# A new order of work on all five engines, and new engines for the casts, in a fused attention and gated feed-forward kernel

## The chip, the cores and the metric

The kernel runs on one core of a Trainium2 chip. A core has five engines, each with its own queue of instructions that it works off strictly in the order in which they were written: TensorE (PE in the profile) for matmuls, VectorE (DVE), ScalarE (ACT), GpSimd (POOL), and SyncE (SP), which here only issues DMAs. Sixteen DMA engines move data between the device memory and the on-chip memory SBUF. Matmuls write into PSUM, a second on-chip memory, from where VectorE or ScalarE must take the results away.

The metric is the device time of one execution in microseconds (us). The kernel before was timed in three runs: 247.0, 247.38 and 248.49 us, median 247.38 us.

## The reference

The inputs are q, k and v of shape (8 batches, 8 heads, 576 positions, 64) in float32, a forget factor f of shape (8, 8, 576), and the weights w_in (512 x 1024), conv_w (3 x 1024) and w_out (1024 x 512).

```python
def _attn_ref(q, k, v, f):
    scale = 1.0 / np.sqrt(D)
    scores = scale * np.matmul(q, k.transpose(0, 1, 3, 2))
    log_f = np.log(np.clip(f, 0.0001, 1.0))
    cum = np.cumsum(log_f, axis=-1)
    decay = cum[:, :, :, None] - cum[:, :, None, :]
    causal = np.triu(np.ones((S, S), dtype=bool), k=1)
    scores = np.where(causal, -1000000000.0, scores + decay)
    scores = scores - np.max(scores, axis=-1, keepdims=True)
    attn = np.exp(scores)
    attn = attn / (np.sum(attn, axis=-1, keepdims=True) + 1e-09)
    return np.matmul(attn, v)

def _moe_ref(x, w_in, conv_w, w_out):
    h = np.maximum(x @ w_in, 0.0)
    hp = np.concatenate([zeros, h, zeros], axis=1)      # one position on each side
    conv_out = sum(conv_w[k] * hp[:, k:k + S, :] for k in range(3))
    gate = 1.0 / (1.0 + np.exp(-conv_out))
    return (h * gate) @ w_out
```

The output of the attention, heads side by side, is the input x of the feed-forward part (FFN). Both are computed for each of the 8 batches.

## The kernel before, in words

The attention is cut into 16 half batches, numbered 0 to 15, of four heads each. The FFN runs per batch, over eight blocks of 128 hidden channels (ff 0 to 7). Everything is written as named tasks, about a thousand of them; a table in the source, ORDER, lists them in one long sequence, and `Plan.play` walks through it and writes the instructions of each task to its engine. So ORDER alone sets the order on each engine's queue, SP's included. A name with an @ behind it also chooses the engine where the kernel allows several (casts of v, casts of the weights, copies out of PSUM).

The tasks, with the half batch or batch as the first number in the name:

- Loads by SP: `ld` loads q and k of half batches 0 and 1 in plain form (L159); `q` loads q or k of half batches 2 to 15 with a transposing DMA (L180, 576 KB in float32, 28 of them); `v` loads v (L209, five pieces a batch); `wi` and `wo` load the weights (L510).
- Casts and small work: `tp` transposes the plain q and k on TensorE (L166) and `cl` takes them from PSUM (L172 on ACT, L174 on DVE); for the transposed loads `cl` clears two of each pair of rows in place (L186 on DVE, half batches 2 to 7). `rw` (L202, L203) or, from half batch 8 on, `fi` (L194, L196) then writes the decay rows into the loaded tile by DMA, from an image that `ki` (L279) made. Only after `rw` or `fi` has landed can the scores of that half batch begin. `va` casts v to float16 (L217, and L219 for its last 64 rows), `wic` and `woc` cast the weights (L518).
- Scores on TensorE: per pair of heads `sd` (diagonal blocks, numbered 2 x half batch and 2 x half batch + 1) and two `so` (the blocks below it), per half batch `st` (the last 64 positions), all L312; where the causal mask is added on TensorE (half batches 0 to 7) a mask matmul (L320) comes first; half batch 0 adds the decay by two more matmuls per block (L315, L317). ScalarE takes the exponentials: `ed` (L353), `eo` (L370), `et` (L332). From half batch 8 on GpSimd sets the masked part to zero: `md` (L356), `mt` (L335).
- `pv` (L389, L394) multiplies with v, in two parts; `n` and `m` on DVE (L403, L405) divide by the row sums; `t` (L414) turns the result on TensorE and `tx` (L417) takes it from PSUM, or a transposing DMA `tx` does both (L420, half batches 11 to 15).
- FFN: `f` (L429) is x @ w_in for one ff; `r` (L440, ACT) the relu; `c` and `d` (L446, L448, DVE) the three-point convolution; `a` (L451, ACT) the gate's tanh or sigmoid; `g` (L458 or L456, DVE) the product; `o` (L474) is the product with w_out; `e` (L479, L484) copies it from PSUM and `s` (L490, L495, L497, L499, L500) stores it.

PSUM holds four buffers (`ps`) that all of these share: a TensorE task that takes one must wait until the engine that reads it out has released one. The loaded q and k lie in a ring of four tiles, so the loads of half batch n wait for the last scores of half batch n-4.

## Time and profile before

| what | before |
|---|---|
| median of 3 runs | 247.38 us (247.0 to 248.49) |
| span of the profiled execution | 244.1 us (244.06 to two places), 6385 instructions |
| median of the runs less that span | 3.3 us |
| PE busy | 226.9 us (93%) |
| ACT busy | 206.9 us (85%) |
| DVE busy | 205.1 us (84%) |
| POOL busy | 52.9 us (22%) |
| DMA queue of SP | 119981 packets, 48.97 MB, 92.4% of 16 engines' span |

The page gives no time of the profiled execution other than its span, from the first instruction to the last; the 3.3 us by which the median of the runs is longer lies around the span. Busy times are sums over one execution; an engine can be busy on work on which nothing waits. The share of the DMA queue is the time that its packets took, against 16 engines for the whole span.

### The profile page before, as it was taken

The numbers are of one execution on the slowest core, as the hardware profiler recorded it, in microseconds if no ns is written. First come the engines' busy times: TensorE is split into PE (matmuls) and PEld (weight loads), VectorE is DVE, ScalarE is ACT, GpSimd is POOL, SyncE is SP. The second block draws the span as 40 slices with busy tenths as digits, with TensorE's granted clock in tenths as the row PEclk, the third lists the DMA queues.
The fourth block names the chain that finished last, engine by engine and source line by source line (L and its number), as shares of the span: only waits on it lengthen the run. The fifth ranks groups of instructions, "written<-read, shape, count | busy, mean of one in ns | idle before, by whom it ended". The sixth has DMA issues, their size and how long they took to land.

```text
span 244.1 us, 6385 instructions
## 1 busy us (share of the span) xinstructions
PE 226.9 (93%) x2627; PEld 145.0 (59%) x2627; DVE 205.1 (84%) x323; ACT 206.9 (85%) x278; POOL 52.9 (22%) x77
## 2 busy tenths in 40 slices
...
GB/s 192 328 159 243 304 204 192 202 253 279 204 188 205 228 158 240 229 314 186 198 256 246 187 209 257 273 134 222 194 260 188 236 140 3 168 157 62 142 86 216
DMA packets 120176, 49.68 MB, mean 204 GB/s; under 512 B 109759, under 2 KB 110271, under 8 KB 120147
## 3 DMA queue, kind: packets, MB, share of 16 engines
q1 hardware_dynamic: 119981, 48.97, 92.4%
...
q10 hardware_dynamic: 166, 0.31, 0.4%
...
HBM read 21.11 MB, written 10.17 MB: 128 GB/s over the span
## 4 chain that ended last, share of the span: by engine, by line
PE 78%; DVE 7%; DMA 6%; ACT 4%; issue 1%; ACTq 1%; SPq 1%; DVEq 0%
PE ps L474 24%; PE ps L429 20%; PE ps L312 15%; PE ps L389 7%; DMA qk<-in_q_dram 3%; PE ps L320 3%; PE ps L394 3%; PE ps L166 2%; PE ps L414 2%; DVE u L446 2%; ACT pp L370 2%; DMA pd<-in_moe_conv_w_dram 2%; DVE u L448 2%; DVE qk L186 1%; DMA qk<-image 1%
## 5 line engine op out<-in xcount | busy, mean ns | idle before, releaser
L429 PE MATMUL ps<-xt,w_in_f 128*128 128x512 f16 (+1 forms) x512 | 69.9, 286 | 0.0
L370 ACT ACTIVATE pp<-ps 128x1024 f16<-128x1024 f32 x64 | 64.7, 1032 | 4.2 <-PE ps L312 2.7
L474 PE MATMUL ps<-w_out_f,hg 128*128 128x512 f16 x288 | 66.8, 379 | 0.0
L312 PE MATMUL ps<-qk 128*128 128x128 bf16 (+2 forms) x576 | 63.4, 240 | 1.6 <-ACT pp L353 0.8
L446 DVE SCALAR_TENSOR_TENSOR u<-ht,cwt 128x576 f32<-128x576 f16 x64 | 52.7, 837 | 3.6 <-ACT ht L440 3.4
L451 ACT ACTIVATE hg<-u,cw 128x576 f16<-128x576 f32 x64 | 48.7, 782 | 5.9 <-DVE u L448 5.8
L448 DVE SCALAR_TENSOR_TENSOR u<-ht,cwt,u 128x576 f32<-128x576 f16 x64 | 53.2, 846 | 0.5
L429 PEld LDWEIGHTS <-w_in_f 128*128 128x128 f16 x512 | 34.3, 98 | 28.5
L312 PEld LDWEIGHTS <-qk 128*128 128x128 bf16 x576 | 39.2, 98 | 19.8 <-issue 3.3
L440 ACT ACTIVATE ht<-ps 128x576 f16<-128x576 f32 x64 | 41.0, 663 | 6.0 <-DVE hg L458 2.7
L474 PEld LDWEIGHTS <-hg 128*128 128x128 f16 x288 | 26.9, 98 | 28.8
L458 DVE SCALAR_TENSOR_TENSOR hg<-hg,ht 128x576 f16<-128x576 f16 x51 | 38.7, 771 | 0.6 <-ACT hg L451 0.5
L356 POOL TENSOR_SCALAR_AFFINE_SELECT pp<-pd 128x1024 f16<-128x1024 f32 x16 | 19.7, 1244 | 53.6 <-ACT pd L353 53.6
L389 PE MATMUL ps<-va,pp 128*128 128x65 f16 x640 | 24.8, 193 | 1.1 <-DVE va L217 1.0
L389 PEld LDWEIGHTS <-pp 128*128 128x128 f16 x640 | 22.6, 97 | 3.7 <-DVE va L217 1.3
L405 DVE TENSOR_TENSOR xm<-ps,rc 128x896 f16<-128x896 f32 (+1 forms) x32 | 23.9, 751 | 0.5
L353 ACT ACTIVATE pp<-ps 128x1024 f16<-128x1024 f32 x16 | 16.6, 1039 | 4.7 <-PE ps L312 3.9
L353 ACT ACTIVATE pd<-ps 128x1024 f32<-128x1024 f32 x16 | 16.2, 1023 | 1.2 <-PE ps L312 1.0
L217 POOL CAST va<-vf 128x1024 f16<-128x1024 f32 x8 | 10.0, 1252 | 32.1 <-DMA vf<-in_v_dram 27.8
L320 PE MATMUL ps<-mask,ident 128*128 128x512 bf16 (+1 forms) x40 | 14.3, 359 | 1.5 <-ACT pp L370 0.8
L403 DVE RECIPROCAL rc<-ps 128x14 f32<-128x14 f32 (+1 forms) x32 | 6.7, 208 | 8.6 <-PE ps L394 5.5
L479 ACT COPY ob<-ps 128x1024 f32<-128x1024 f32 (+1 forms) x14 | 12.9, 919 | 0.3 <-issue 0.2
...
## 6 DMA issues: line engine op xcount, KB each, us to landing
...
```

What stands on the lines that cost most here:

```text
L312: nc.tensor.matmul(o, tk[:, h * S + k0:h * S + k0 + 128], tq[:, h * S + q0:h * S + q0 + n], start=first, stop=last and not by_matmul(hb, h))
L353: nc.scalar.activation(o, ps_of(f"sd{i}").rearrange("p (s c) -> p s c", s=2), AF.Exp, scale=SCALE)
L370: nc.scalar.activation(pair(i)[:, s, 512:1536], ps_of(f"so{i}.{s}"), AF.Exp, scale=SCALE)
L389: nc.tensor.matmul(ps[:, c:c + D + 1], block(hb, h, m, n), va[:, h, m, 0:D + 1], start=(m == 0), stop=(m == n))
L405: nc.vector.tensor_tensor(xm[:, CUT * D * u:CUT * D * u + nj * k * D].rearrange("p (j x d) -> p j x d", x=k, d=D), got[:, :, :, 0:D], r.un ...
L429: nc.tensor.matmul(ps[:, t0:t1], w_in_f16[:, cc, 128 * ff:128 * (ff + 1)], xt[:, cc // 2, x:x + t1 - t0], start=(cc == 0), stop=(cc == NCC ...
L440: nc.scalar.activation(ht_of(b, ff)[:, 2:2 + S], ps_of(f"f{b}.{ff}")[:, 0:S], AF.Relu, scale=1.0 if (b, ff) in LATE else 0.5)
L446: nc.vector.scalar_tensor_tensor(u, ht[:, 1:1 + S], cwt[:, ff, 0:1], ht[:, 2:2 + S], op0=ALU.mult, op1=ALU.add)
L448: nc.vector.scalar_tensor_tensor(u, ht[:, 3:3 + S], cwt[:, ff, 1:2], u, op0=ALU.mult, op1=ALU.add)
L451: nc.scalar.activation(hg_of(b, ff), u_t[slot[f"c{b}.{ff}", "u"]], AF.Sigmoid if (b, ff) in LATE else AF.Tanh, scale=cw[:, ff, 1:2])
L458: nc.vector.scalar_tensor_tensor(hv, hv, 1.0, ht_of(b, ff)[:, 2:2 + S], op0=ALU.add, op1=ALU.mult)
L474: nc.tensor.matmul(ps[:, 512 * (c % 2):512 * (c % 2 + 1)], w, w_out_f16[:, ff, :], start=(ff == 0), stop=(ff == NFF - 1))
```

## The change

Only the table ORDER changes. It holds the same 1054 tasks, and each task does what it did. Their sequence is new throughout, and 39 tasks of a free choice run on another engine:

| kind of task | before | after |
|---|---|---|
| `va`, 128 x 1024 | POOL 8, ACT 4, DVE 4 | POOL 13, ACT 1, DVE 2 |
| `va`, 64 x 256 | POOL 6, ACT 6, DVE 4 | POOL 12, ACT 1, DVE 3 |
| `wic`, `woc` | POOL 8 | POOL 6, ACT 1, DVE 1 |
| `cl` of half batches 0 and 1 | ACT 5, DVE 3 | ACT 7, DVE 1 |
| `tx` from PSUM | DVE 9, ACT 2 | DVE 10, ACT 1 |
| `e`, 1024 wide | ACT 11, DVE 3 | ACT 13, DVE 1 |
| `e`, 512 wide | ACT 6, DVE 2 | ACT 6, DVE 2 |

The diff is one line of the table for another; its beginning:

```diff
 ORDER = """
-dca cw ld0 ld1 ld0.0.0 tp0.0.0 dcl ld0.1.0 ld0.0.1 tp0.0.1 tp0.1.0 v0.0 ld0.1.1 ld1.0.1 ld1.0.0 dcs dck v0.1 v0.2 v0.3 v0.4
...
+ld0 ld1 ld0.0.1 ld1.0.0 ld0.0.0 ld1.0.1 tp1.0.0 dca q2.1 tp0.0.0 tp1.0.1 tp0.0.1 dcl cl0.0.1@ACT ld0.1.0 cl1.0.1@ACT cl0.0.0@ACT
...
 """
```

What this does to the queues is shown at three places.

**The start of ScalarE's queue.** The rows follow the logarithm of f and its table load. qk_85 and qk_86 are the tiles of half batches 0 and 1; L172 is `cl`, L353 `ed`, L370 `eo`. Before:

```order
L172 ACTIVATE qk_85<-ps_130,lim 128x1152
L172 ACTIVATE qk_85<-ps_131,lim 128x1152
L172 ACTIVATE qk_85<-ps_132,lim 128x1152
L353 ACTIVATE pp_95<-ps_131 128x2x512
L370 ACTIVATE pp_95<-ps_132 128x1024
L370 ACTIVATE pp_95<-ps_131 128x1024
```

And after the change:

```order
L172 ACTIVATE qk_85<-ps_132,lim 128x1152
L172 ACTIVATE qk_86<-ps_131,lim 128x1152
L172 ACTIVATE qk_85<-ps_130,lim 128x1152
L172 ACTIVATE qk_86<-ps_131,lim 128x1152
L172 ACTIVATE qk_86<-ps_132,lim 128x1152
L172 ACTIVATE qk_86<-ps_129,lim 128x1152
L353 ACTIVATE pp_95<-ps_130 128x2x512
L172 ACTIVATE qk_85<-ps_129,lim 128x1152
L370 ACTIVATE pp_95<-ps_130 128x1024
```

Three casts stood ahead of the first exponential; now six do, four of them for half batch 1, and a seventh follows.

**SP's queue between the decay rows of two half batches.** qk_86, qk_87 and qk_88 are the tiles of half batches 5, 6 and 7 here; L202 and L203 together are one `rw`. Before, from `rw5` to the beginning of `rw6`:

```order
L202 DMA qk_86<-image 1x2304
L203 DMA qk_86<-image 2x2304
L510 DMA ob_128<-in_moe_w_out_dram 128x2x512
L180 DMA_TRANSPOSE qk_87<-in_q_dram 128x2304
L180 DMA_TRANSPOSE qk_87<-in_k_dram 128x2304
L180 DMA_TRANSPOSE qk_88<-in_q_dram 128x2304
L180 DMA_TRANSPOSE qk_88<-in_k_dram 128x2304
L209 DMA vf_90<-in_v_dram 128x8x64 x2
L202 DMA qk_87<-image 1x2304
```

After, the stretch that ends with `rw6`; the rows before the first L202 are a load for half batch 5, a piece of v, and the first load for half batch 6:

```order
L180 DMA_TRANSPOSE qk_86<-in_q_dram 128x2304
L209 DMA vf_89<-in_v_dram 128x8x64
L180 DMA_TRANSPOSE qk_87<-in_q_dram 128x2304
L202 DMA qk_86<-image 1x2304
L203 DMA qk_86<-image 2x2304
L209 DMA vf_89<-in_v_dram 128x8x64 x2
L180 DMA_TRANSPOSE qk_87<-in_k_dram 128x2304
L209 DMA vf_89<-in_v_dram 128x8x64
L180 DMA_TRANSPOSE qk_88<-in_q_dram 128x2304
L202 DMA qk_87<-image 1x2304
L203 DMA qk_87<-image 2x2304
```

The transposing loads stood four in a row; now a plain load stands between two of them nearly everywhere, and all four loads of w_out come behind `rw6`, where three of them stood ahead of `rw5` and one behind it.

**The end of SP's queue.** The stores of the last two batches; L490 and the last L497 (or L499 with L500) belong to batch 7. Before:

```order
L495 DMA out_dram<-ob_126 128x2x512
L495 DMA out_dram<-ob_125 128x2x512
L499 DMA out_dram<-ob_128 64x512
L500 DMA out_dram<-ob_128 64x512
L490 DMA out_dram<-ob_127 128x512 x2
L490 DMA out_dram<-ob_126 128x512 x2
```

After:

```order
L495 DMA out_dram<-ob_128 128x2x512
L495 DMA out_dram<-ob_125 128x2x512
L490 DMA out_dram<-ob_126 128x512
L490 DMA out_dram<-ob_127 128x512 x2
L490 DMA out_dram<-ob_126 128x512
L497 DMA out_dram<-ob_128 128x512
```

The last store was one of 256 KB behind two copies out of PSUM; now it is the last block of the batch, in one DMA, behind one copy.

2 lines of the change are left out of this document (1 added, 1 removed).

## The prediction

> **What bounds the kernel now.** I read the page's busy times first, then the table of stretches, then the chain that ended last, then SP's queue.
>
> ```profile
> PE 226.9 (93%) x2627; PEld 145.0 (59%) x2627; DVE 205.1 (84%) x323; ACT 206.9 (85%) x278; POOL 52.9 (22%) x77
> ...
> 0.00:10.00 10.00, 2.83 (x27) 2.85 (x28) 5.69 (x23) 3.98 (x4) 5.37 (x31) 1.00 0.85 243
> ...
> 20.00:30.00 10.00, 8.82 (x111) 6.29 (x109) 4.25 (x5) 7.30 (x10) 3.06 (x3) 1.00 0.97 275
> ...
> 40.00:60.00 20.00, 16.67 (x247) 11.51 (x246) 19.79 (x30) 19.47 (x28) 4.29 (x4) 1.00 1.11 242
> 60.00:100.00 40.00, 39.99 (x485) 25.72 (x483) 38.17 (x57) 38.20 (x54) 5.52 (x5) 1.00 1.06 204
> ...
> 230.00:244.00 14.00, 8.66 (x41) 3.72 (x38) 4.82 (x9) 4.73 (x7) 0.00 (x0) 0.99 0.39 132
> ```
>
> Columns of a stretch: length, then busy time (and instructions) of PE, weight loads, DVE, ACT, POOL, then TensorE's granted clock, the DMA share and GB/s. PE is busy 226.9 of 244.06 us. Its idle 17.2 us lie in four places: 7.17 us before 10 us, 1.18 in 20 to 30, 3.33 in 40 to 60, and 5.34 at the end. From 60 us until the last matmul PE has no hole worth naming, at a granted clock of 1.00. So a new order of the same matmuls can win or lose in the first 60 us and at the tail, or lose by new holes behind.
>
> A busy PE need not be a fast one, so I price the tasks by the chain, where pieces follow each other without overlap:
>
> ```profile
> 33.81 0.50 PE ps L414 x9
> ...
> 60.32 0.22 PE ps L320
> 60.54 0.22 PE ps L312 x4
> ...
> 62.18 0.44 PE ps L312 x4
> 62.62 0.98 PE ps L429 x8
> ...
> 69.25 1.73 PE ps L474 x8
> ...
> 77.48 0.99 PE ps L389 x32
> ...
> 83.30 0.44 PE ps L394 x20
> 83.74 0.32 PE ps L320
> ```
>
> Prices: `t` and `tp` 0.50, `so` 0.44, a masked `sd` 4 x 0.22 = 0.88, `f` 0.98, `o` 1.73, `pv` 0.99 and 0.69 (eight L389 at a quarter of 0.99, and 0.44). 83.74 is `sd13`, the first score of half batch 6. PE's work ahead of it: 15.0 for what both orders open with (eight `tp` 4.0, the weights of the convolution 0.9, half batch 0 with three matmuls where others have one 10.1), ten masked `sd` 8.8, twenty `so` 8.8, five `st` 1.1, `pv` 0 to 4 and half of 5 9.4, four `t` 2.0, sixteen `f` 15.7, four `o` 6.9: together 67.7. **PE's lag**, the clock less the work done, is 83.7 - 67.7 = 16.0 us there, and hardly grows until the end. The forecast is a forecast of this lag and of the tail.
>
> What made the lag? In 40 to 60 us ACT (19.47 of 20) and DVE (19.79) are full and PE is not. SP's queue is the other suspect:
>
> ```profile
> 54.81 6.16 SPq L209 DMA_DIRECT2D vf<-in_v_dram  x4
> ...
> 62.15 0.38 SPq L202 DMA_DIRECT2D qk<-image  x1
> ...
> 63.77 3.96 SPq L180 DMA_TRANSPOSE qk<-in_q_dram  x1
> ...
> 77.27 1.14 SPq L209 DMA_DIRECT2D vf<-in_v_dram  x2
> ...
> 85.65 6.12 SPq L180 DMA_TRANSPOSE qk<-in_k_dram  x2
> ...
> 96.95 0.95 SPq L194 DMA_DIRECT2D qk<-blank  x1
> ...
> 115.29 4.33 SPq L180 DMA_TRANSPOSE qk<-in_k_dram  x2
> ```
>
> SP issues without a gap. Four transposing loads took 77.27 - 63.77 = 13.5 us, four others 96.95 - 85.65 = 11.3 us: 2.8 to 3.4 us each, and 2.2 us where nothing held them back (4.33 for two). Four pieces of v took 6.16, 1.5 each. So the transfers are a queue nearly as full as PE, and what an order puts ahead of a needed one is paid.
>
> **The change, part by part.** (1) *The start.*
>
> ```profile
> GB/s 0 28 288 311 210 306 262 271 357 394 390 308 228 218 217 165 183 4 198 292 122 286 256 244 250 296 330 301 346 321 138 186 286 162 212 256 110 79 290 228
> ...
> 9.26 3.72 ACT L172 ACTIVATE qk<-ps,lim 128x1152 uint16<-128x1152 uint16 x3
> ...
> 11.83 0.38 PE L320 MATMUL ps<-mask,ident 128*128 128x512 bf16 x1
> ...
> 22.71 3.01 DMA qk<-image
> ```
>
> The first line gives what the DMAs moved in each of the first 40 us; its first nine slices add up to 2.03 MB. Before, `sd0` (11.83) waited for the first plain loads and three casts on ACT, 3.72 us. After, the first cast needs `tp0.0.1`, which stands behind `tp1.0.1` on PE, and so four loads of 1.77 MB beside the 0.29 MB of f: about 9 us, plus two turns, 10.2 us. Six casts at 1.24 end at 17.7, and `sd0` can begin after the third, at about 14. Half batch 1 then needs `rw1`; its image DMA took 3.01 us. Behind the casts that is 17.7 + 3.5, and with one more transposing load ahead of it in SP's queue up to 23, against 25.7 before. But PE has then done only 11.4 us (`tp` 4.0, two `sd` and three `so` of half batch 0 7.4), so the lag is 22.5 - 11.4 = 11 already: the earlier decay rows win nothing, since PE's other work was put behind them. **No lag below 11 us is to be had.**
>
> (2) *The decay rows of half batch 6.* After, PE's work ahead of `sd12` is 15.0 + ten `sd` 8.8 + twenty `so` 8.8 + four `st` 0.9 + `pv` 0 to 3 and half of 4 7.7 + four `t` 2.0 + eleven `f` 10.8 = 54.0: five `f`, four `o` and some `pv` less than before, so q, k and v are needed earlier against the clock. In SP's queue `rw6` has ahead of it what `rw5` had (issued at 62.15), plus three transposing loads and one `rw` (1.0), less one piece of v (1.5) and three loads of w_out; such a load costs between 0.5 (its issue below) and 1.3 us (512 KB at the best slice, 394 GB/s).
>
> ```profile
> 23.45 1.43 SPq L510 DMA_DIRECT2D ob<-in_moe_w_in_dram  x3
> ```
>
> With 2.8 us for a transposing load: 62.15 + 8.4 + 1.0 - 1.5 - (1.5 to 3.9), 66.2 to 68.5, and 3.5 until landed: 69.7 to 72.0, middle 70.8; lag 16.8. With 3.4 us: up to 73.8, lag 19.8. With 2.2 us for all eleven (6.6 for the three, and eight older ones 0.8 cheaper each by the 3.0 that they had): 6 to 8 us earlier, and the start's 11 to 12 us rule. I take 2.8, the price of the less crowded four, since the change puts plain loads between: **+0.8 us** of lag, with ends -4 and +3.8.
>
> The DMA: Bandwidth & Descriptors page of the Trainium skill (section Latency and other measured facts) gives a DMA transpose 261 GB/s, so by an estimate 590 KB would take 2.3 us. By that the lag would be the start's, the faster rival's. The trace's 2.8 to 3.4 us speak against it in runs of four.
>
> (3) *Engines of casts.*
>
> ```profile
> L479 ACT COPY ob<-ps 128x1024 f32<-128x1024 f32 x11 | 11.0, 1003 | 0.3 <-issue 0.2
> ...
> L172 ACT ACTIVATE qk<-ps,lim 128x1152 uint16<-128x1152 uint16 x5 | 6.3, 1308 | 0.1
> ...
> L174 DVE TENSOR_SCALAR qk<-ps,lim 128x1152 uint16<-128x1152 uint16 x3 | 4.4, 1477 | 4.7 <-PE ps L166 4.6
> L217 ACT CAST va<-vf 128x1024 f16<-128x1024 f32 x4 | 4.3, 1074 | 0.0
> ...
> L479 DVE COPY ob<-ps 128x1024 f32<-128x1024 f32 x3 | 3.7, 1218 | 2.0 <-ACT xt L417 1.9
> L217 DVE CAST va<-vf 128x1024 f16<-128x1024 f32 x4 | 3.6, 908 | 0.4 <-DMA out_dram<-ob 0.4
> ...
> L219 ACT CAST va<-vf 64x256 f16<-64x256 f32 x6 | 2.4, 408 | 0.0
> ```
>
> DVE loses two big `va` (1.8), two `cl` (3.0) and two `e` (2.4) and gains a weight cast (0.9) and a `tx` (0.8): -5.5 us of 205. ACT loses three big and five small `va` (3.2 + 2.0) and a `tx` (about 1.1), and gains two `cl` (2.6), a weight cast (1.1) and two `e` (2.0): -0.6. POOL gains five big and six small `va` and loses two weight casts. The price at the end is 0 as long as PE is full behind 60 us; without that cover DVE's 5.5 us would count.
>
> ```profile
> 65.26 1.50 POOL L217 CAST va<-vf 128x1024 f16<-128x1024 f32 x1 [4.25 <-PE ps L429]
> ...
> 65.05 0.81 DVE L446 SCALAR_TENSOR_TENSOR u<-ht,cwt 128x576 f32<-128x576 f16 x1
> 66.37 1.00 DVE L446 SCALAR_TENSOR_TENSOR u<-ht,cwt 128x576 f32<-128x576 f16 x1 [0.51 <-ACT ht L440]
> ...
> 16.53 1.04 POOL L217 CAST va<-vf 128x1024 f16<-128x1024 f32 x1 [10.07 <-DMA vf<-in_v_dram]
> ```
>
> A cast on POOL takes 1.04 alone and 1.50 where DVE's L446 began 0.2 us ahead of it, and the next L446 ran 0.19 longer while the cast ended: each makes the other wait. Eleven casts more, at 1.04 (and some 0.4 for a small one), less two, can hold DVE up by 5.5 us at most: DVE's gain is then gone, no more. The SBUF — State Buffer page of the Trainium skill (section SBUF: two separate sides) calls the port pair that the two share an exclusive lock, the loser fully blocked; the rows agree, and by that rule the sum stays as it is.
>
> (4) *The tail.*
>
> ```profile
> 226.41 12.25 PE L474 MATMUL ps<-w_out_f,hg 128*128 128x512 f16 x56
> ...
> 238.69 1.07 ACT L484 COPY ob<-ps 128x512 f32<-128x512 f32 x2 [0.45 <-PE ps L474]
> ```
>
> Behind the last matmul two copies stand on ACT (1.07), then a store. After, one copy of the last block does: **-0.5 us**. -0.7 if the smaller store lands sooner; 0 if `e7.3` is late and pushes `e7.4`.
>
> **Sum**, against the profiled execution: 244.06 + 0.8 - 0.5 = 244.4 us of span. The median of the runs lies 3.3 us above the span of the profile before, so 247.7 us: no change that can be told.
>
> **Rivals.** *A, the forecast*: the lag is 15 to 18 and the time 245 to 249.8. *B, faster*: a transposing load with plain loads behind it costs near 2.2 us, and the full queues of 40 to 60 us are spread, since the new order brings half batches 3 to 5 ahead of much of the FFN of batch 0. For it: 2.2 us occurs, and the runs of four are what is broken up. Against it: the start's 11. Lag 12.5, 3.5 less than now, and the tail: 247.4 - 4.0 = 243.4 us. *C, slower*: `rw6` (and with the same arithmetic `fi8` and `fi10`) comes late, because a transposing load ahead of it that half batch 6 doesn't need (`q7.0`) delays it in SP's strict order, and PE waits at `sd12`. It decides from 3.2 us a load; at 3.4 the lag is 19.8: 247.4 + 3.8 - 0.5 = 250.7 us. For it: SP has no gap to catch up in, and PE is ahead of the clock by less work. *D, the change doesn't do what it says*: the mutual waits of GpSimd and DVE aren't removed but multiplied by the 25 casts there, and reach PE through a late `m` or `va`. If half of the 5.5 us gets through: 250 us. Against it: DVE is relieved by as much.
>
> **Chances.** A 0.42, B 0.31, C 0.21, D 0.06. Faster by over 1% (below 244.9) is B, 0.31; slower by over 1% (above 249.9) is C and D, 0.27; within 1%, about what a measurement here can tell from no change, 0.42. The range goes from somewhat below B's time to above C's, as the ends of step 2 are far apart: 242.2 to 252.0; A's own is 245 to 249.8.
>
> **What would show it.** The stretch 0 to 10 with PE still near 3 us busy; `sd0` at about 14; the first L312 of half batch 1 at 21.5 to 23; SP without gaps and `rw6` issued at 66 to 69; PE full from about 72 us; no L484 pair behind the last matmul. The prediction is wrong if PE shows holes behind 75 us (a new wait, on ACT's or DVE's order or a late `va`), or if `rw6` is issued before 63.

## The result and the profile after

| | before | after |
|---|---|---|
| median | 247.31 us (247.0 to 248.49, 4 runs) | 265.89 us (264.46 to 267.09, 4 runs) |
| span of the profiled execution | 244.06 us | 262.7 us |
| DVE's busy time until 60 us, and behind it | 41.34 and 163.74 us | 29.08 and 182.82 us |

The ratio is 1.073, 95% interval 1.067 to 1.079: **7% slower**, far outside the range of 242.2 to 252.0. The same quantity as in the prediction, PE's lag (the clock less the work done, by the prediction's prices), shows when it happened: 19.2 us at 60 us (before 15.4), 26.6 at 100 (15.9), 29.5 at 150 (16.1), 35.5 at 220 (16.5). So 3.8 us were lost in the first 60 us and 15.2 more behind them, in the part where the prediction held PE to be full. Medians and ratios here and below leave out runs in a slower state of the chip, one of experiment 10 (255.61 us) and four of before. The kernel before, timed anew beside the experiments, had medians of 247.1 to 248.0 us, so differences below some 1 us tell nothing.

First the busy times of the page, the shares of the chain that ended last by engine, and the table of stretches of after (columns as in the prediction):

```profile
PE 234.4 (89%) x2627; PEld 148.3 (56%) x2627; DVE 211.9 (81%) x318; ACT 208.6 (79%) x274; POOL 63.6 (24%) x86
PE 40%; DVE 26%; ACT 10%; DMA 9%; SPq 8%; issue 4%; POOL 2%; DVEq 0%; ACTq 0%; POOLq 0%
...
0.00:60.00 60.00, 47.84 (x612) 36.46 (x613) 29.08 (x61) 44.10 (x49) 13.61 (x41) 0.97 1.00 210
60.00:262.00 202.00, 186.57 (x2018) 111.80 (x2014) 182.82 (x258) 164.48 (x225) 49.95 (x45) 0.99 0.82 184
...
60.00:80.00 20.00, 18.59 (x224) 12.21 (x221) 19.93 (x30) 18.54 (x25) 3.40 (x3) 1.00 0.80 188
80.00:100.00 20.00, 17.26 (x193) 10.36 (x191) 17.73 (x24) 13.78 (x19) 5.52 (x6) 0.91 0.95 217
100.00:120.00 20.00, 18.05 (x212) 11.04 (x211) 19.67 (x26) 17.06 (x25) 5.58 (x6) 1.00 1.12 200
```

and of before the chain's shares and the stretches, cut in the same way:

```profile
PE 78%; DVE 7%; DMA 6%; ACT 4%; issue 1%; ACTq 1%; SPq 1%; DVEq 0%
...
0.00:60.00 60.00, 48.32 (x671) 36.66 (x672) 41.34 (x79) 45.98 (x55) 16.17 (x42) 1.00 1.07 236
60.00:244.00 184.00, 178.55 (x1959) 108.36 (x1956) 163.74 (x245) 160.94 (x224) 36.76 (x36) 1.00 0.89 193
```

What is to be seen: PE was busy as long until 60 us (47.84 against 48.32, of it 3.41 us at half clock after the change), but **DVE 12.3 us less**. In the three stretches from 60 us on DVE is 89 to 100% busy (19.93, 17.73 and 19.67 of 20) while PE has holes (18.59, 17.26, 18.05), and the chain that ended last runs through DVE for 26% of the span instead of 7%. The last matmul ended at 238.7 before and at 257.7 after. From 60 us to there DVE was busy for 163.74 of 178.7 us before, 92%, and for 182.82 of 197.7 after, 92% again. DVE has 19.1 us more to do behind 60 us, and the span is 18.6 us longer. That suggests DVE, but busy time alone doesn't show what PE waited for; the waits and the experiments below test it.

Why had it 19.1 us more? 12.3 were left over from the first 60 us. The other 6.8 are a longer sum, 211.9 against 205.1, although casts and copies worth 5.5 us were taken from it. The groups of DVE's three long element operations (count, then busy us and mean ns of one), before and then after:

```profile
L448 DVE SCALAR_TENSOR_TENSOR u<-ht,cwt,u 128x576 f32<-128x576 f16 x64 | 53.2, 846 | 0.5
L446 DVE SCALAR_TENSOR_TENSOR u<-ht,cwt 128x576 f32<-128x576 f16 x64 | 52.7, 837 | 3.6 <-ACT ht L440 3.4
L458 DVE SCALAR_TENSOR_TENSOR hg<-hg,ht 128x576 f16<-128x576 f16 x51 | 38.7, 771 | 0.6 <-ACT hg L451 0.5
```

```profile
L448 DVE SCALAR_TENSOR_TENSOR u<-ht,cwt,u 128x576 f32<-128x576 f16 x64 | 57.0, 907 | 0.7
L446 DVE SCALAR_TENSOR_TENSOR u<-ht,cwt 128x576 f32<-128x576 f16 x64 | 55.8, 886 | 5.4 <-ACT ht L440 5.3
L458 DVE SCALAR_TENSOR_TENSOR hg<-hg,ht 128x576 f16<-128x576 f16 x51 | 44.9, 892 | 2.0 <-ACT hg L451 1.8
```

The same 179 instructions take 157.7 us instead of 144.6. The timeline of after shows where (start, duration; the operations of the two engines alone):

```profile
183.41 1.65 POOL L217 CAST va<-vf 128x1024 f16<-128x1024 f32 x1 [7.71 <-DVE hg L458]
184.09 1.59 DVE L448 SCALAR_TENSOR_TENSOR u<-ht,cwt,u 128x576 f32<-128x576 f16 x1
185.02 1.61 POOL L356 TENSOR_SCALAR_AFFINE_SELECT pp<-pd 128x1024 f16<-128x1024 f32 x1
...
188.45 1.61 POOL L356 TENSOR_SCALAR_AFFINE_SELECT pp<-pd 128x1024 f16<-128x1024 f32 x1
189.03 1.64 DVE L458 SCALAR_TENSOR_TENSOR hg<-hg,ht 128x576 f16<-128x576 f16 x1
```

An L448 takes 1.59 and an L458 1.64 beside an operation of POOL, and that one 1.6. Alone (no POOL operation beside them) they took 0.81 and 0.75 on average in both traces, and a mask L356 as little as 1.09. Of after's L448, nine had at least 0.7 us of POOL beside them, and these took 1.46 on average. By the POOL operation beside them, L446, L448, L458 and L186 ran longer than alone by: casts of v (L217, L219) 5.5 us, masks L356 8.9, casts of the weights 4.1, small masks 0.9; 19.4 in all. Before, the same sum was 5.2, of it 1.7, 1.2, 1.3 and 1.0. So the masks, which the change neither added nor gave to another engine, cost most. Before, the 16 masks ran beside L446, L448 or L458 for 5.8 of their 19.9 us and beside L405 for 5.6; after, for 16.2 of 22.1 us and for 2.5. L405 takes its large operand from PSUM, and its longer form took the same 1.09 beside a mask as alone:

```profile
132.73 1.09 DVE L405 TENSOR_TENSOR xm<-ps,rc 128x896 f16<-128x896 f32 x1
133.06 1.10 POOL L356 TENSOR_SCALAR_AFFINE_SELECT pp<-pd 128x1024 f16<-128x1024 f32 x1 [3.45 <-ACT pd L353]
```

(before's timeline.)

How DVE's lateness reaches PE is seen in what PE waited for in after (us in total, times, longest):

```profile
...
PE ps L429 <- ACT ht L440: 2.8, 4, 1.7
PE ps L312 <- DVE xm L405: 2.7, 2, 1.4
PE ps L389 <- POOL va L217: 2.2, 1, 2.2
PE ps L414 <- DVE xm L405: 1.5, 2, 0.8
...
PE ps L389 <- DVE xm L405: 1.3, 1, 1.3
PE ps L429 <- DVE xm L405: 1.1, 2, 0.7
```

Against the 0.8 us that PE waited for L405 before, it is 6.6 now: a late `m` (L405) holds one of the four PSUM buffers, and PE's next task wants it. The single wait for `va`, 2.2 us, is `pv3.0` at 52 us; there GpSimd had itself stood idle for 2.99 us, until v landed for the cast, so the loss of the first 60 us began with a load.

Behind 60 us PE's waits of more than 0.15 us add up to 10.7 us: 6.6 for L405, 2.8 for the relu L440 and 1.2 for exponentials, none for decay rows. ScalarE was late in part because of DVE: behind 60 us it waited 12.1 us for L448 and 4.6 us for L458. From 92.5 us on PE also ran for 3.41 us at half its clock, which costs 1.7 us more. That is 12.4 of the 16.3 us by which the lag grew between 60 and 220 us (in before it grew by 1.1); where the rest went was not found.

### The profile page after: what moved, and what is told of

Read it like the earlier page. It is cut to its first block, busy times and chain, and to the rows that moved or that the text cites. A ratio compares the mean times of both kernels' runs of the same rounds, so it can differ in the third digit from the quotient of the medians.

```text
span 262.7 us, 6382 instructions
## 1 busy us (share of the span) xinstructions
PE 234.4 (89%) x2627; PEld 148.3 (56%) x2627; DVE 211.9 (81%) x318; ACT 208.6 (79%) x274; POOL 63.6 (24%) x86
## 4 chain that ended last, share of the span: by engine, by line
PE 40%; DVE 26%; ACT 10%; DMA 9%; SPq 8%; issue 4%; POOL 2%; DVEq 0%; ACTq 0%; POOLq 0%
PE ps L474 14%; PE ps L429 9%; DVE u L446 6%; DVE u L448 6%; PE ps L312 6%; DVE hg L458 6%; DVE xm L405 4%; PE ps L389 3%; DMA vf<-in_v_dram 3%; SPq L180 3%; DMA hg<-in_k_dram 3%; ACT hg L451 3%; SPq L209 2%; DMA ob<-in_moe_w_out_dram 2%; DVE qk L186 2%
## 5 line engine op out<-in xcount | busy, mean ns | idle before, releaser
L429 PE MATMUL ps<-xt,w_in_f 128*128 128x512 f16 (+1 forms) x512 | 72.1, 288 | 5.4 <-ACT ht L440 2.8
L370 ACT ACTIVATE pp<-ps 128x1024 f16<-128x1024 f32 x64 | 64.1, 1027 | 6.4 <-PE ps L312 5.8
L312 PE MATMUL ps<-qk 128*128 128x128 bf16 (+2 forms) x576 | 65.0, 243 | 3.8 <-DVE xm L405 2.7
L446 DVE SCALAR_TENSOR_TENSOR u<-ht,cwt 128x576 f32<-128x576 f16 x64 | 55.8, 886 | 5.4 <-ACT ht L440 5.3
L451 ACT ACTIVATE hg<-u,cw 128x576 f16<-128x576 f32 x64 | 48.0, 774 | 12.4 <-DVE u L448 12.1
L448 DVE SCALAR_TENSOR_TENSOR u<-ht,cwt,u 128x576 f32<-128x576 f16 x64 | 57.0, 907 | 0.7
L429 PEld LDWEIGHTS <-w_in_f 128*128 128x128 f16 x512 | 35.1, 98 | 35.5 <-issue 7.4
L312 PEld LDWEIGHTS <-qk 128*128 128x128 bf16 x576 | 39.9, 99 | 21.1 <-issue 5.1
L440 ACT ACTIVATE ht<-ps 128x576 f16<-128x576 f32 x64 | 41.2, 655 | 12.2 <-PE ps L429 6.3
L458 DVE SCALAR_TENSOR_TENSOR hg<-hg,ht 128x576 f16<-128x576 f16 x51 | 44.9, 892 | 2.0 <-ACT hg L451 1.8
L474 PEld LDWEIGHTS <-hg 128*128 128x128 f16 x288 | 26.8, 98 | 29.4 <-DVE hg L456 0.3
L217 POOL CAST va<-vf 128x1024 f16<-128x1024 f32 x13 | 16.6, 1286 | 68.2 <-DMA vf<-in_v_dram 43.5
L356 POOL TENSOR_SCALAR_AFFINE_SELECT pp<-pd 128x1024 f16<-128x1024 f32 x16 | 22.0, 1380 | 30.3 <-ACT pd L353 30.2
L405 DVE TENSOR_TENSOR xm<-ps,rc 128x896 f16<-128x896 f32 (+1 forms) x32 | 24.0, 752 | 0.5
L353 ACT ACTIVATE pp<-ps 128x1024 f16<-128x1024 f32 x16 | 16.3, 1025 | 3.1 <-PE ps L312 2.2
L353 ACT ACTIVATE pd<-ps 128x1024 f32<-128x1024 f32 x16 | 16.5, 1029 | 1.3 <-PE ps L312 1.2
L186 DVE TENSOR_SCALAR qk<-qk,lim 128x2304 uint16<-128x2304 uint16 x12 | 11.1, 928 | 6.3 <-DMA qk<-in_q_dram 5.3
L479 ACT COPY ob<-ps 128x1024 f32<-128x1024 f32 (+1 forms) x15 | 14.3, 952 | 2.0 <-PE ps L474 1.8
L166 PE MATMUL ps<-ident_b,hg 128*128 128x128 bf16 x72 | 7.8, 287 | 8.8 <-DMA hg<-in_q_dram 6.9
```

The costliest lines, as they stand in the source:

```text
L312: nc.tensor.matmul(o, tk[:, h * S + k0:h * S + k0 + 128], tq[:, h * S + q0:h * S + q0 + n], start=first, stop=last and not by_matmul(hb, h))
L353: nc.scalar.activation(o, ps_of(f"sd{i}").rearrange("p (s c) -> p s c", s=2), AF.Exp, scale=SCALE)
L370: nc.scalar.activation(pair(i)[:, s, 512:1536], ps_of(f"so{i}.{s}"), AF.Exp, scale=SCALE)
L405: nc.vector.tensor_tensor(xm[:, CUT * D * u:CUT * D * u + nj * k * D].rearrange("p (j x d) -> p j x d", x=k, d=D), got[:, :, :, 0:D], r.un ...
L429: nc.tensor.matmul(ps[:, t0:t1], w_in_f16[:, cc, 128 * ff:128 * (ff + 1)], xt[:, cc // 2, x:x + t1 - t0], start=(cc == 0), stop=(cc == NCC ...
L440: nc.scalar.activation(ht_of(b, ff)[:, 2:2 + S], ps_of(f"f{b}.{ff}")[:, 0:S], AF.Relu, scale=1.0 if (b, ff) in LATE else 0.5)
```

## The experiments

Two theories at the start: **S, sharing** (GpSimd's new casts hold DVE up) and **O, order** (DVE's work was put late and it can't catch up). A third, **T, transfers** (SP's order of loads), came in with the later runs; its counterpart there, **V**, is DVE's owed work and sharing together. To thin an operation means to let it work on fewer columns; order and engines stay.

**1 and 2: order and engines apart.** The edit is in ORDER alone: the order of the one kernel, the engines behind the @ of the other.

```
- ... cl0.1.1@ACT ... va4.0@POOL ... va4.1@POOL ... va7.0@POOL ...      (after)
+ ... cl0.1.1@DVE ... va4.0@ACT  ... va4.1@DVE  ... va7.0@DVE  ...      (each task as before has it)
```

> The changed order with each cast given back to the engine that it had before (40 tags; no task moves in the order). Theory S, sharing: GpSimd's eleven more casts of v hold VectorE up (its three long element operations of the FFN grew by 13.1 us in sum, 144.6 to 157.7), and that is what makes the change slow; then this kernel gets most of it back: 250 to 255 us. Theory O, order: VectorE's work was put late (by 60 us it had done 12 us less of its own work than before), and it never catches up; then the engines hardly matter: 262 to 269 us, since VectorE and ScalarE get casts back.

> The order of before with the 40 tags of after: GpSimd does eleven more casts of v, nothing else moves. Theory S: 256 to 260 us, since the casts cost VectorE some 12 us wherever they stand. Theory O: 246 to 250 us, since the casts fall beside work that does not mind, or into VectorE's slack.

Measured: 273.62 us (ratio to before 1.106, 1.102 to 1.111) and 277.73 us (1.124, 1.119 to 1.129). Both theories missed. Each half of the change alone is slower than the whole. In the second, PE stood still for 10.9 us at one place. It waited for an exponential (L370), and that stood on ACT behind a cast of w_in (`wic1`, L518), which after's tag gives to ACT and which waited 10.20 us for its load:

```profile
PE ps L320 <- ACT pp L370: 11.4, 2, 10.9
...
26.61 1.04 ACT L518 CAST w_in_f<-ob 128x1024 f16<-128x1024 f32 x1 [10.20 <-DMA ob<-in_moe_w_in_dram]
```

So an order and its engines are one solution, and to move all 40 tags at once tells nothing of the casts of v.

**3 and 4: the first 60 us apart from the rest.** The tasks that had begun by 60 us in the trace of one kernel, then the rest as the other has it.

```
  ORDER = (tasks of before that began by 60 us, in its order) + (all others, in after's order)
  ORDER = (tasks of after that began by 60 us, in its order) + (all others, in before's order)
```

> All tasks that had begun by 60 us in the trace of before, in the order and on the engines of before; then the rest in the order and on the engines of after (8 tasks wait for a free buffer and go a few places back). Theory O: the 12 us that VectorE lost by 60 us, and the hole of TensorE at 52 us with the half clock behind it, are gone: 249 to 254 us. Theory S: the sharing behind 60 us stays, and only the hole's 4 us go: 259 to 263 us.

> The mirror: all tasks that had begun by 60 us in the trace of after, in its order and on its engines; then the rest as before. Theory O: VectorE starts the rest 12 us behind and keeps TensorE waiting: 257 to 262 us. Theory S: only the hole at 52 us is paid: 250 to 253 us.

Measured: 267.27 us (1.082, 1.077 to 1.087) and 259.48 us (1.047, 1.041 to 1.054). The second is as O expected. Its stretches (columns as above):

```profile
60.00:80.00 20.00, 14.13 (x133) 8.82 (x133) 17.12 (x25) 12.29 (x19) 5.96 (x5) 0.83 1.10 240
80.00:100.00 20.00, 19.85 (x251) 12.82 (x249) 18.82 (x30) 18.47 (x26) 1.91 (x2) 1.00 0.68 146
100.00:120.00 20.00, 20.00 (x271) 13.29 (x270) 19.90 (x31) 19.37 (x28) 0.97 (x1) 1.00 1.09 248
```

The lag is 17.1 us at 60 us, 26.8 at 80 and 27.8 at 220: what the start left undone (DVE had 32.3 us busy by then, before 41.3) is paid within 20 us, and before's rest then loses next to nothing. From 60.2 to 65.8 us the chain of that run is DVE's work with hardly a break, so here it is DVE that PE waited for; of the 9.7 us, 3.4 are a stretch of 6.83 us at half clock behind that hole.

The first gained nothing at all: with before's start its lag is 15.7 at 60 us and 28.0 at 90. But what it lost there is not DVE's:

```profile
60.00:70.00 10.00, 5.90 (x46) 3.57 (x45) 4.84 (x5) 5.59 (x7) 2.23 (x2) 0.76 0.90 166
70.00:85.00 15.00, 12.07 (x112) 7.26 (x110) 9.06 (x10) 10.26 (x13) 4.54 (x4) 0.84 0.91 205
```

DVE was busy for 13.90 of these 25 us. PE's seven waits were for exponentials on ACT (5.5 us in sum) and decay rows (1.6), and 10.24 us at half clock cost 5.1 more: 12.1 of the 12.3. So the sequence that was joined here stalls by its scores and exponentials, and this run says nothing of DVE's work, for or against.

**5: GpSimd thinned.**

```
-        if part == 0:
+        if e == "POOL" and hb >= 4:
+            va, vf = va[:, :, :, 0:2], vf[:, :, :, 0:2]
...
-        nc.gpsimd.affine_select(... all four blocks of the diagonal
+        nc.gpsimd.affine_select(... [:, :, 0:1] ... pattern=[[0, 2], [0, 1], [1, 128]]
```

> After, with GpSimd's casts of v from half batch 4 on cut to 2 of 64 columns and its masks of half batches 8 to 15 to a quarter (so these parts of v are left uncast and three quarters of the diagonal unmasked); order and engines unchanged. After's VectorE operations beside such casts and masks ran 14.3 us longer in sum than the same operations alone. Theory S, sharing: those 14 us are what TensorE waits for behind 60 us: 250 to 256 us. Theory O, order: VectorE owes 12 us of its own work at 60 us, and sharing is a smaller part: 258 to 263 us. Sharing worthless: 264 to 267 us.

Measured: 259.06 us (1.046, 1.040 to 1.052), 6.8 us less than after, between S and none, where O put it. DVE's extra time beside POOL fell from 19.4 to 6.8 us. A thin cast also ends sooner, so `pv` and the buffer of v gain as well; this run doesn't part the two.

**6 and 7: only the casts of v.** The 18 casts of v from half batch 4 on whose engine differs, with the tags of the other kernel.

```
- va5.0@POOL va4.0@ACT va5.1@ACT va4.1@DVE va7.0@DVE va7.1@ACT va8.0@ACT ...
+ va5.0@DVE va4.0@POOL va5.1@POOL va4.1@POOL va7.0@POOL va7.1@POOL va8.0@DVE ...
```

> The order of before; only the 18 casts of v from half batch 4 on whose engine the change altered are on after's engine (GpSimd has 7 more of them from there on, DVE and ACT fewer). The rest, above all the opening's casts of q and k, as before. Theory S by number of casts: 252 to 257 us. Theory S by place (a cast or mask costs VectorE only beside its operations that read and write SBUF alone) and theory O: 246 to 251 us.

> The mirror: after, with these 18 casts on before's engine. Theory S by number of casts: 255 to 261 us. By place, and theory O: 263 to 270 us, since the masks do most of the sharing and VectorE gets casts back.

Measured: 249.38 us (1.007, 1.004 to 1.010) and 265.16 us (1.069, 1.064 to 1.074; after is 1.073). From half batch 4 on, the headline of the change, more casts on GpSimd, is worth under 1% either way; the earlier casts, `va3.0` of the hole at 52 us among them, were not in these runs. In before's order the casts raise DVE's extra time from 5.2 to 9.3 us, and some 1.5 us of that show in the time; in after's order, giving them back saves DVE 2.7 us of extra time and costs it the casts.

**8: DVE's work cut.**

```
+        if b < 3:
+            h2 = S // 2
+            nc.vector.scalar_tensor_tensor(hv[:, 0:h2], hv[:, 0:h2], 1.0, ht_of(b, ff)[:, 2:2 + h2], ...
```

> After, with the gate of VectorE (L458) over half of its columns in batches 0 to 2 (the other half of the FFN's hidden rows is left without its gate): 24 operations less by some 0.37 us, 9 us, from 62 to 137 us, where VectorE is full in the stretches. If VectorE's pace is what TensorE waits for there: 256 to 259 us. If ScalarE, the loads or TensorE's own order set the pace: 263 to 266 us.

Measured: 265.21 us (1.069, 1.064 to 1.074): no gain that can be told, in the range given for a pace set by ScalarE, the loads or PE's order. DVE's busy time fell by 6.5 us (211.9 to 205.4), less than the 9 expected. The lag shows what became of them: it was 26.7 us at 150 us (after 29.5), so some 3 us did get through; then it jumped to 30.8 at 152 to 156 us, by a wait of 2.25 us and 3.41 us at half clock behind it, and met after's (36.1 against 35.5 at 220). `sd24`, the first score of half batch 12, waited for its decay rows, a DMA from SP's queue, and in the run with GpSimd thinned the same task waited for them, too. PE's timeline of the two runs:

```profile
152.18 0.90 PE L312 MATMUL ps<-qk 128*128 128x128 bf16 x8 [2.25 <-DMA qk<-image]
```

```profile
150.32 0.61 PE L318 MATMUL ps<-qk 128*128 128x128 bf16 x8 [2.46 <-DMA qk<-image]
```

(L318 is L312 there.) So the decay rows, and with them the loads, stand close behind DVE: hence theory T.

**9 and 10: the loads cut.**

```
         t = t[hb % RING]
+        nh = 2 if hb >= 6 else nh
         nc.sync.dma_start_transpose(
```

> After, with every transposing load of q and k from half batch 6 on moving two of its four heads (the other two heads of these half batches keep old data); order and engines unchanged. It halves 20 loads that took 2.7 to 6.9 us of SP's queue each. Theory T, transfers: SP's queue in after's order is what holds TensorE up behind 60 us (it waited for the decay rows of half batch 7 until 93 us, the thinned run for those of half batch 12 until 150): 250 to 257 us. Theory V, VectorE: it owes work and is held up by GpSimd: 262 to 266 us.

> Both thinnings at once, the half loads and GpSimd's casts and masks of the earlier run (259.06 us). If the two are walls one behind the other: 246 to 252 us, of which 3 us over before's lag were lost in the first 60 us. If VectorE alone is the wall: 257 to 260 us, as without the half loads.

Measured: 262.23 us (1.056, 1.049 to 1.062) and 252.27 us (1.018, 1.012 to 1.023). Alone the half loads give 3.7 us, on top of the thin GpSimd 6.8: together 13.6, against the 10.5 of the two apart. **Walls of nearly the same height**, limits of which one shows only when the other is lowered, would behave like that; but the surplus, 0.011 in the ratios, is no larger than its uncertainty (each of the four ratios is known to 0.005 to 0.007), so it is not shown. With both, the lag is 22.8 us at 100 and 23.4 at 220: behind 100 us nothing is lost any more.

**11 and 12: the list of transfers exchanged.** SP's list of the one kernel, all else as the other has it but for the tasks that would stand ahead of their load.

```
- ... v2.2 q7.0 rw6 wo3 v2.4 wo2 wo0 wo1 q7.1 ...        (after, SP)
+ ... rw5 wo2 q6.0 q6.1 q7.0 q7.1 v3.0 v3.1 rw6 ...      (before, SP)
```

> After, with SP's whole list in the order of before; TensorE's order as after's but for 2 places, ScalarE's, VectorE's and GpSimd's moved in 21, 41 and 6 places, where a task would have stood ahead of its load. Theory T: 252 to 260 us. Theory V: 263 to 270 us.

> The mirror: before, with SP's list in the order of after; TensorE's order unchanged, ScalarE, VectorE and GpSimd moved in 7, 4 and 5 places. Theory T: 254 to 262 us. Theory V: 246 to 251 us.

Measured: 296.51 us (1.196, 1.188 to 1.204) and 292.61 us (1.180, 1.173 to 1.187), far beyond what either theory gave. In the first PE waited 26.2 us for decay rows:

```profile
PE ps L312 <- DMA qk<-image: 26.2, 5, 8.0
```

Neither list is bad in itself; one that doesn't match the order of the work costs some 30 to 45 us. In the second it waited most for casts of the weights on GpSimd (8.2 and 4.2 us). Both stall on the exchange itself, so these two runs don't tell T from V.

**13 to 16: control, and the pieces.** In order: both thinnings in the kernel before; only the masks thinned in after; only the casts of v; both thinnings and the half gate. The edits are those above.

> Control: the kernel before with both thinnings (half loads from half batch 6 on, GpSimd's casts of v from half batch 4 on and its masks cut). Its TensorE has no hole behind 60 us, so if the thinnings act only through such holes, 246 to 248 us. If they speed any order: 238 to 243 us.

> After with the masks alone cut to a quarter. By place: in after's profile VectorE's long operations beside the 16 masks ran 8.9 us longer in sum (1.2 before), so most of the 6.8 us goes: 258 to 261 us. By number of casts: 264 to 266 us.

> After with GpSimd's casts of v from half batch 4 on alone cut. By place: VectorE ran 5.5 us longer beside all of its casts of v (1.7 before): 262 to 265 us. By number of casts: 258 to 261 us.

> After with both thinnings and VectorE's gate over half of its columns in batches 0 to 2 as well. If the lag that is left behind 60 us (18.8 to 22.8 us by 100 us, then flat) is VectorE's owed work: 248.5 to 250.5 us. If it is something else, such as the order of ScalarE's work: 252 to 254 us.

Measured: 246.96 us (0.997, 0.993 to 1.000) for the control, so **the thinnings gain nothing where PE has no holes**: what they gain in after is the change's loss. Masks alone 262.27 us (1.062, 1.054 to 1.071), casts alone 260.66 us (1.053, 1.046 to 1.060): both count, 3.6 and 5.2 us. The split by place, most of it for the masks, was wrong. A thin cast also ends earlier for `pv` and frees the buffer of v for SP's next load, which may be why; no run tests that. All three thinnings: 250.46 us (1.012, 1.006 to 1.018), just inside the range for DVE's owed work, with 18.3 us of lag at 60, 21.1 at 100 and 21.7 at 220. The stretches of that run:

```profile
60.00:120.00 60.00, 58.25 (x713) 37.66 (x708) 53.61 (x88) 54.91 (x76) 9.93 (x15) 1.00 0.94 189
120.00:180.00 60.00, 59.92 (x709) 37.91 (x708) 51.68 (x81) 56.88 (x78) 11.99 (x22) 1.00 0.85 186
```

against the same two of after:

```profile
60.00:120.00 60.00, 53.90 (x625) 33.60 (x622) 57.33 (x78) 49.38 (x67) 14.51 (x14) 0.97 0.96 202
120.00:180.00 60.00, 58.16 (x708) 37.52 (x707) 55.83 (x81) 54.10 (x73) 18.64 (x16) 1.00 1.06 218
```

PE is nearly full again, with DVE less busy.

Taken off one by one, the 18 us are: GpSimd's part 6.8 (265.9 to 259.1), the loads 6.8 (to 252.3), some of DVE's own work 1.8 (to 250.5; its busy time fell by 8.7 us, 200.2 to 191.5), and 2.8 over the 247.6 of before. The thinned run still has 2.4 us more lag than the control at 60 us (18.3 against 15.9), which is nearly that. The first two steps are clear of noise, the third is not. The amounts can depend on the order of taking off. **Shown** is that most of the loss goes through GpSimd's operations and the transposing loads of the later half batches: to thin both gives back 13.6 of the 18 us here, and under 1 us in before. **Left open:** how much DVE's 12 us of late work cost by themselves; how much of GpSimd's part is DVE held up, and how much a late v; how much of the loads' 6.8 us is SP's order and how much is that SP itself waits, for tiles and buffers that a late PE, DVE or POOL frees.

## Why the prediction was wrong, by its steps

- **"The price at the end is 0 as long as PE is full behind 60 us"** is the step that failed: PE was not full there. The prediction did name the other way out, to "lose by new holes behind", and then priced it only as late decay rows (C) and as half of 5.5 us through `m` or `va` (D). The runs showed 10.7 us of waits behind 60 us, 6.6 of them for `m` on DVE and 4.0 for ACT, and a lag that grew there by 16.3 us. PE's own stretches were right for before; but DVE (38.17 of 40 us) and ACT stood in the same row, and full engines next to a full PE are walls, not cover. The prediction counted what PE had done at each point of the new order, and what SP had ahead of it, and never did the same sum for DVE. It would have found most of the 12 us: after's opening scores and exponentials of half batches 3 to 5 carry no work for DVE, and the FFN that does was put behind them. With that sum alone, an estimate made after the fact with the measured 29.1: DVE's 205.1 - 5.5 - 29.1 = 170.5 us behind 60, at before's 92% (0.917) 186 us, 60 + 186 + 5 + 3.3 = 254 us.
- **Step 3, the casts: 0, and at most 5.5 us.** Wrong in size and in kind. It counted the added casts alone, five at 1.04 us and six at 0.4 less two of the weights, which gives its 5.5. Measured, DVE's extra time rose by 14.2 us (5.2 to 19.4), and most of the rise is by masks and weight casts that the change only moved, 1.2 to 8.9 and 1.3 to 4.1. The rows that it quoted (1.50 and 1.04, 0.19 longer) were a light case: had each been blocked until the other's end, the cast would have been 0.60 us longer and not 0.46, the next L446 0.39 and not 0.19. They agree with a lock in direction, not in amount. 1.46 for 0.81 is the usual case where the two overlap by 0.7 us. Adding 14.2 / 0.917 to the 254 above gives some 270, a little above the 265.9 measured; this sum is made after the fact and none of its parts was tested alone.
- **Rival D** had the mechanism, "through a late `m` or `va`", with a chance of 0.06 and 250 us. Half of 5.5 us was the mis-sized term: L405 alone held PE up for 6.6 us.
- **Step 2 and rival C, late decay rows.** Half right. `rw6` was issued at 71.2 to 73.5 (forecast 66 to 69), and `sd12` began at 74.7, a lag of 20.7 (forecast 16.8; C said 19.8). But most of that lag was there already, from `pv3.0` at 52 us. `rw7` was late, too: its load `q7.1` stood at SP for 6.93 us, `cl7` on DVE came at 87.88 and 89.67, `rw7` at 88.77 to 91.17, and half batch 7 began at 94.4. Yet PE's waits of that stretch were for L405 and a relu, and none behind 60 us was for decay rows, so C's mechanism was not what was paid.

```profile
76.57 6.93 SPq L180 DMA_TRANSPOSE qk<-in_k_dram  x1
...
87.88 0.86 DVE L186 TENSOR_SCALAR qk<-qk,lim 128x2304 uint16<-128x2304 uint16 x1
88.77 0.25 SPq L202 DMA_DIRECT2D qk<-image  x1
89.67 0.86 DVE L186 TENSOR_SCALAR qk<-qk,lim 128x2304 uint16<-128x2304 uint16 x1
90.56 0.61 SPq L203 DMA_DIRECT2D qk<-image  x1
```

- **Rival B, 2.2 us a load once plain loads stand between.** The other way round. The 28 transposing loads stood 3.16 us each at SP before and 3.86 after, 19.7 us more in sum. In three of before's four runs of four the first is the dearest (4.9, 2.7, 2.1, 2.2 at 108 to 120 us; in the run at 86 us it is the second); broken up by plain loads, more of them are a first (5.0 and 4.4 at 114 and 120), which may be why. The times may hold waits for a tile as well. The estimate of 2.3 us a load was below both means.
- **Step 1, the start.** Nearly right: stretch 0 to 10 with 2.67 us of PE busy (near 3), `sd0` at 15.5 (about 14), the lag 13.4 at 20 to 30 us (11 was called the floor). Half batch 1's first L312 came at 25.4 (forecast 21.5 to 23), hardly earlier than before's 25.8, but PE came to it from other work, without a wait for `rw1`.
- **Step 4, the tail.** Right: one copy on ACT behind the last matmul, and 5.05 us from its end to the end of the span against 5.4.

```profile
254.68 2.97 PE L474 MATMUL ps<-w_out_f,hg 128*128 128x512 f16 x13
...
257.73 0.59 ACT L484 COPY ob<-ps 128x512 f32<-128x512 f32 x1 [0.19 <-ACT ob L484]
```

The prediction's own sign of error came true: "PE shows holes behind 75 us (a new wait, on ACT's or DVE's order or a late `va`)".
